# PSUM read-outs in streams of their own, and column tiles behind the scores, in a two-layer infini-attention kernel

## The chip, the cores and the metric

The kernel runs on one core of one Trainium2 chip. PSUM is the memory into which TensorE writes its products; it is divided into banks, and a bank is free for the next product when VectorE or ScalarE has read it out. The metric is device time in microseconds (us), the median over single executions. An execution counts as slow only where it is over 1.5% above the fastest of its kernel; the granted clock of TensorE is given with every execution. **Ratios** in this document are the mean time of one kernel's fast runs over the mean time of the fast runs of the kernel before in the same rounds on the same chip, with a 95% interval. They are therefore not quite the ratio of the medians quoted beside them. "Span" is the length of the one profiled execution, about 2 us shorter than its device time.

## The reference, cut to what matters

Two layers, each an attention with a compressive memory and a feed-forward part, over 2048 tokens of width 640; 32 heads of 20 columns, four segments of 512 tokens.

```python
for s in range(N):                                   # 4 segments
    logits = einsum('bhqd,bhkd->bhqk', qs, ks) * scale + mask
    p = softmax(logits)
    a_dot = einsum('bhqk,bhkd->bhqd', p, vs)          # scores, exponential, application
    pq = phi(qs)
    a_mem = einsum('bhld,bhde->bhle', pq, M) / (einsum('bhld,bhd->bhl', pq, z) + 1e-6)   # memory read
    outs.append(g * a_mem + (1 - g) * a_dot)
    M = M + einsum('bhld,bhle->bhde', phi(ks), vs)    # memory update
...
x = x + A(layernorm(x));  x = x + B(layernorm(x))     # B: relu(x @ w1) @ w2, width 1728
x = x + A(layernorm(x));  x = x + B(layernorm(x))
```

## The kernel before

The kernel's program is written as streams (Python generators): scores, exponentials, projections, feed-forward and so on. While the program is **built**, a small time model picks the next instruction of all streams, so the order on every engine is fixed before anything runs. TensorE has three tilings: "rows" for scores, "full" for a 128x128 product, and "cols" for the same product as four 128x32 column tiles. Which of the last two a product gets is decided here:

```python
def _mode(self, op):
    if op.cols is None:                  # scores: rows; application: cols; by token: full
        return op.mode
    return self.mode if self.mode != "rows" else "full"
...
if e == "pe":
    op.mode = self._mode(op)
    self.mode = op.mode
    if op.mode == "cols" and op.cols is not None:
        fns = op.cols                    # four matmuls instead of one
```

The model also charges a change of tiling (`SWITCH_NS = 96.0`) and, in full mode, ranks the application of the probabilities as if it came due 1.5 us after its inputs (`COLS_LAG`), so that it is put off. A product and its read-out from PSUM belong to one stream; the stream goes on when the read-out is recorded:

```python
def ffn(b, s):
    ...
    for dc in range(NFULL):
        bk, tk = yield from group(MISC, L, [(w1_r[:, k, ...], feat(xt, k)) for k in range(FC)], ...)
        th = yield evac(512, 1, ...relu on VectorE..., ...or on ScalarE..., [tk] + HT.tks)
        bk.release(th)
        hr.append(th)
```

Data that changes its layout goes over DMA: scores' operands (`pad<-scr`), and transposes such as `otk<-otu`, `phk<-phs`, `xnT<-xn_tok`, all issued from SyncE.

The softmax here doesn't subtract the row's maximum and nothing guards it: scores larger than these inputs give would overflow.

## Time and profile before

| | before |
|---|---|
| median, range | 557.86 us (557.83 to 558.56) |
| span of the profiled execution | 556.4 us |
| TensorE busy | 98%, 90% of the chain that ended last |
| matmuls, all instructions | 8,158, 18,717 |
| changes of tiling | 338 |

TensorE is busy in every slice, so what counts is the price of its stream and the holes in it. The prediction shows those lines. The page's DMA queues of the kernel before (packets, MB, share of the time of 16 DMA engines):

```profile
q1 hardware_dynamic: 129504, 59.62, 50.1%
...
q8 instruction: 64, 1.05, 0.8%
```

q8 fetches instructions: 64 packets of 16.4 KB. Their share, 0.8% of 16 x 556.4 us, is 71 us, so one packet holds one of the 16 DMA engines for about 1.1 us.

### The profile page before, as it was taken

The numbers are of one execution on the slowest core, as the hardware profiler recorded it, in microseconds if no ns is written. First come the engines' busy times: TensorE is split into PE (matmuls) and PEld (weight loads), VectorE is DVE, ScalarE is ACT, GpSimd is POOL, SyncE is SP. The second block draws the span as 40 slices with busy tenths as digits, with TensorE's granted clock in tenths as the row PEclk, the third lists the DMA queues.
The fourth block names the chain that finished last, engine by engine and source line by source line (L and its number), as shares of the span: only waits on it lengthen the run. The fifth ranks groups of instructions, "written<-read, shape, count | busy, mean of one in ns | idle before, by whom it ended". The sixth has DMA issues, their size and how long they took to land.

```text
span 556.4 us, 18717 instructions
## 1 busy us (share of the span) xinstructions
PE 546.7 (98%) x8158; PEld 307.7 (55%) x8158; DVE 414.3 (74%) x1063; ACT 405.9 (73%) x513; POOL 192.1 (35%) x302
## 2 busy tenths in 40 slices
PE   8998999999999999999999999999999999999998
PEld 7454554445554555645456554565465644657756
DVE  5967989979999988898577988779966588417102
ACT  5699888888777887787898887888774887541140
POOL 5345344433444434344334443244410433301000
PEclk9999999999999999999999999999999999999999
DMA  8596999845563427456187532771319311453101
GB/s 272 138 227 158 221 193 208 233 67 96 103 152 72 89 39 162 96 92 93 39 177 135 85 44 77 176 138 21 68 41 199 103 34 27 97 80 50 52 4 49
DMA packets 130003, 61.30 MB, mean 110 GB/s; under 512 B 108802, under 2 KB 119810, under 8 KB 129922
## 3 DMA queue, kind: packets, MB, share of 16 engines
q1 hardware_dynamic: 129504, 59.62, 50.1%
q8 instruction: 64, 1.05, 0.8%
q10 hardware_dynamic: 418, 0.49, 0.3%
q14 instruction: 17, 0.14, 0.1%
HBM read 20.57 MB, written 12.85 MB: 60 GB/s over the span
## 4 chain that ended last, share of the span: by engine, by line
PE 90%; DMA 4%; DVE 2%; ACT 1%; SPq 1%; issue 0%; POOL 0%; ACTq 0%; POOLq 0%
PE ps L645 45%; PE ps L648 24%; PE ps L1147 9%; PE ps L1241 6%; DMA otk<-otu 2%; PE ps L1280 1%; PE ps L1027 1%; DMA scr<-stg 1%; PE ps L1084 1%; PE ps L625 1%; ACT PT L1209 1%; PE ps L1421 1%; DMA pad<-scr 1%; DMA beta_bc<-in_A_beta_dram 1%; SPq L943 0%
## 5 line engine op out<-in xcount | busy, mean ns | idle before, releaser
L1209 ACT ACTIVATE PT<-ps 128x1024 bf16<-128x1024 f32 x320 | 309.3, 1027 | 66.2 <-PE ps L1147 62.9
L1221 POOL TENSOR_SCALAR_AFFINE_SELECT PT<-PT 128x512 bf16<-128x512 bf16 x256 | 166.7, 669 | 266.6 <-ACT PT L1209 266.5
L1363 DVE TENSOR_TENSOR x_sb<-x_sb,ps 128x320 bf16<-128x320 bf16 x128 | 60.8, 481 | 64.7 <-PE ps L648 47.1
L645 PE MATMUL ps<-w_r,hT 128*128 128x320 bf16 x511 | 82.2, 300 | 0.0
L645 PE MATMUL ps<-xnT,w_r 128*128 128x512 bf16 x262 | 65.7, 380 | 0.0
L1147 PE MATMUL ps<-pad 20*128 20x512 bf16 (+3 forms) x1024 | 63.4, 301 | 1.6 <-DMA pad<-scr 0.8
L648 PE MATMUL ps<-xnT,w_r 128*32 128x512 bf16 x1032 | 62.8, 379 | 0.8 <-issue 0.6
L645 PEld LDWEIGHTS ps<-w_r,hT 128*128 128x128 bf16 x511 | 47.6, 98 | 24.3 <-issue 6.8
L666 DVE BATCH_NORM_STATS2 stats<-x_sb 128x6 f32<-128x320 bf16 x124 | 55.4, 469 | 2.6 <-DMA x_sb<-in_A_x_dram 2.4
L648 PE MATMUL ps<-w_r,hT 128*32 128x320 bf16 x1284 | 49.2, 299 | 0.0
L1147 PEld LDWEIGHTS ps<-pad 20*128 20x128 bf16 x1024 | 17.9, 92 | 52.7 <-ACT PT L1209 26.9
L1450 ACT ACTIVATE hT<-ps 128x512 bf16<-128x512 f32 x50 | 30.0, 600 | 21.4 <-PE ps L648 20.4
L1448 DVE TENSOR_SCALAR hT<-ps 128x512 bf16<-128x512 f32 x54 | 37.0, 686 | 10.0 <-PE ps L645 6.6
L1241 PE MATMUL ps<-PT,v_aug 128*21 128x128 bf16 (+3 forms) x896 | 40.4, 301 | 0.0
L648 PEld LDWEIGHTS ps<-xnT,w_r 128*32 128x32 bf16 x1032 | 26.6, 97 | 22.8 <-issue 0.8
L648 PEld LDWEIGHTS ps<-w_r,hT 128*32 128x32 bf16 x1284 | 33.7, 97 | 9.7 <-DVE x_sb L1363 0.3
L1251 DVE CAST otu<-ps 128x512 bf16<-128x512 f32 x47 | 32.1, 684 | 8.5 <-PE ps L1241 8.1
L645 PEld LDWEIGHTS ps<-xnT,w_r 128*128 128x128 bf16 x262 | 23.4, 97 | 26.3 <-issue 3.5
L682 POOL TENSOR_TENSOR rstd<-lnU,mhalf 128x2 f32<-128x2 f32 (+2 forms) x26 | 20.4, 784 | 47.0 <-DVE lnU L678 37.5
L992 ACT ACTIVATE stg<-stg 128x512 bf16<-128x512 bf16 x50 | 31.6, 634 | 4.0 <-DVE rtmp L990 4.0
L645 PE MATMUL ps<-wo_r,oT 128*128 128x320 bf16 x202 | 32.3, 300 | 0.4 <-DVE x_sb L1363 0.4
L843 DVE CAST stg<-ps 128x512 bf16<-128x512 f32 x39 | 26.4, 683 | 7.8 <-PE ps L645 7.3
(108 smaller groups left out, 725.1 us busy)
## 6 DMA issues: line engine op xcount, KB each, us to landing
pad<-scr SPq DMA_DIRECT2D x124, 80.0 KB
scr<-stg SPq DMA_DIRECT2D x34, 256.0 KB, 2.7
out_dram<-x_sb SPq DMA_DIRECT2D x16, 160.0 KB, 2.0
w_r<-in_B_w_dram SPq DMA_DIRECT2D x10, 216.0 KB, 2.6
w_r<-in_B_w_dram SPq DMA_DIRECT2D x13, 160.0 KB, 2.8
x_sb<-in_A_x_dram SPq DMA_DIRECT2D x10, 160.0 KB, 3.4
scr<-w_r SPq DMA_DIRECT2D x5, 256.0 KB, 2.8
wv_r<-in_A_wv_dram SPq DMA_DIRECT2D x1, 800.0 KB, 8.8
```

The lines of the kernel that those rows point to most:

```text
L645: return e.matmul(view(dst.ap, b), a, b, start=(k == 0), stop=(k == last))
L648: return e.matmul(view(dst.ap[rows], b), part, b, start=(k == 0), stop=(k == last))
L666: tk = yield dve(320, 1, lambda e, c2=c2: e.bn_stats(stats6[:, t % 12, c2, :], x_sb[:, t, c2 * 320:(c2 + 1) * 320]), xt)
L992: te = yield act(512, lambda e, q=q: e.activation(q, q, ACT.Exp), [tr] + p, psum=False)
L1147: fns.append([(lambda e, z=z, j=j, hh=hh, N=N, o=o, sl=sl, q=hh % 2: e.matmul(slot.ap[:, q, o:o + N], sl.ap[32 * hh:32 * hh + DH, z, 0, 12 ...
L1209: tx = yield act(1024, lambda e, dst=dst, src=src: e.activation(dst, src, ACT.Exp, scale=SCALE), sc + pw)
L1221: tm = yield pool(600.0, lambda e, reg=reg: e.affine_select(out=reg, in_=reg, pattern=[[0, 4], [1, 128]], compare_op=ALU.is_ge, fill=0.0, ...
L1241: fns.append((lambda e, OD, j=j, hh=hh: e.matmul(OD.ap[32 * hh:32 * hh + DH + 1, 128 * j:L], VAUG[vx(a, s)][:, j, 4 * g + hh, :], pt.ap[:, ...
L1251: te = yield evac(L, 1, lambda e: e.tensor_copy(dst, OD.ap), lambda e: e.activation(dst, OD.ap, ACT.Copy), [tk] + OTU[0].tks)
L1363: ta = yield dve(320, 1, lambda e: e.tensor_tensor(x_sb[:, t, 320 * hf:320 * hf + 320], x_sb[:, t, 320 * hf:320 * hf + 320], bk.ap[:, 0:32 ...
L1448: th = yield evac(512, 1, lambda e, dc=dc, bk=bk: e.tensor_scalar(hT[:, dc, :], bk.ap[:, :], 0.0, None, ALU.max), lambda e, dc=dc, bk=bk: ...
L1450: lambda e, dc=dc, bk=bk: e.activation(hT[:, dc, :], bk.ap[:, :], ACT.Relu), [tk] + HT.tks)
```

## The change

The intent: with read-outs in streams of their own, a second product group can go into another bank while the first is being read out; and with cols behind scores, TensorE no longer turns from full to cols within one stretch between two score blocks. The core of the diff:

```diff
@@ _mode
-        return self.mode if self.mode != "rows" else "full"
+        return self.mode if self.mode != "rows" else "cols"
@@ _settle
+            if isinstance(y, Spawn):
+                self.add(y.prio, y.gen)
+                self.rank[id(y.gen)] = self.rank[id(st[1])]
+                st[2], st[3] = None, (None,)
@@ ffn
+            def square(dc, bk, tk):
+                th = yield evac(512, 1, ...)
+                bk.release(th)
+                S.set("hr", b, s, dc, tks=[th])
             for dc in range(NFULL):
+                if dc >= 2:
+                    yield Need(*hr[dc - 2])
                 bk, tk = yield from group(MISC, L, ...)
-                th = yield evac(512, 1, ...)
-                bk.release(th)
-                hr.append(th)
+                yield Spawn(6, square(dc, bk, tk))
```

Left out: the same for the query and key projections (`proj_part`), the values (`proj_v`) and the residual add behind the second feed-forward product. Projections and values may be two groups ahead only from the fourth segment on.

More of the change, by code (lines that the diff above doesn't have):

```diff
@@ L156, in __init__ @@
         self.key = key
+class Spawn:
+    def __init__(self, prio, gen):
+        self.prio = prio
+        self.gen = gen
 LONE_NS = 300.0
@@ L214, in _settle @@
                 return True
-            if isinstance(y, Need):
+            if isinstance(y, Spawn):
+                self.add(y.prio, y.gen)
+                self.rank[id(y.gen)] = self.rank[id(st[1])]
+                st[2], st[3] = None, (None,)
+            elif isinstance(y, Need):
                 if y.key not in self.events:
@@ L281, in run @@
                 moved = False
-                for st in self.streams:
+                for st in list(self.streams):
                     had, ended = st[2], st[4]
@@ L641, in group @@
             for k, (a, b, *w) in enumerate(mms):
-                w = list(w[0]) if w else []
+                if w and isinstance(w[0], Need):
+                    w = yield w[0]
+                else:
+                    w = list(w[0]) if w else []
                 def mm(e, dst, k=k, a=a, b=b):
@@ L842, in proj_part, with settle @@
                 (w_r[:, k, c * 128:(c + 1) * 128], feat(xt, k)[:, i0:i1]) for k in range(FC)], w)
-            te = yield evac(N, 1, lambda e, sg=sg, bk=bk: e.tensor_copy(sg.ap[:, t0:t0 + N], bk.ap[:, 0:N]),
-                            lambda e, sg=sg, bk=bk: e.activation(sg.ap[:, t0:t0 + N], bk.ap[:, 0:N], ACT.Copy),
-                            [tk] + sg.tks)
-            bk.release(te)
-            ev.append(te)
-            if len(ev) == (1 if h is None else 2):
-                S.set("stg", a, s, c, n, tks=ev)
+            def settle():
+                te = yield evac(N, 1, lambda e: e.tensor_copy(sg.ap[:, t0:t0 + N], bk.ap[:, 0:N]),
+                                lambda e: e.activation(sg.ap[:, t0:t0 + N], bk.ap[:, 0:N], ACT.Copy), [tk] + sg.tks)
+                bk.release(te)
+                ev.append(te)
+                S.set("qkpart", a, s, c, n, h)
+                if len(ev) == (1 if h is None else 2):
+                    S.set("stg", a, s, c, n, tks=ev)
+            yield Spawn(5, settle())
             return tk
@@ L854, in proj_first @@
             order += [(c, n, None) for c in range(2, FC) for n in range(2)]
-            for c, n, h in order:
+            for z, (c, n, h) in enumerate(order):
+                if z >= 1:
+                    c0, n0, h0 = order[z - 1]
+                    yield Need("qkpart", 0, 0, c0, n0, h0)
                 tk = yield from proj_part(0, 0, c, n, h)
@@ L865, in f @@
                 for c in range(FC):
+                    back = 2 if (a, s) >= (0,3) else 1
+                    if c >= back:
+                        yield Need("qkpart", a, s, c - back, n, None)
                     tk = yield from proj_part(a, s, c, n, None)
@@ L885, in proj_v, with settle @@
             done = []
+            def settle(i, hf, bk, tk):
+                dst = va.ap[:, i, 16 * hf:16 * hf + 16, 0:DH]
+                src = bk.ap[:, 0:320].rearrange("p (h e) -> p h e", e=DH)
+                te = yield evac(320, 1, lambda e: e.tensor_copy(dst, src), lambda e: e.activation(dst, src, ACT.Copy),
+                                [tk] + va.tks)
+                bk.release(te)
+                done.append(te)
+                S.set("vpart", a, s, 2 * i + hf)
+                if len(done) == 8:
+                    S.set("v", a, s, tks=done)
             for i in range(4):
@@ L888, in proj_v @@
                 for hf in range(2):
+                    back = 2 if (a, s) >= (0,3) else 1
+                    if 2 * i + hf >= back:
+                        yield Need("vpart", a, s, 2 * i + hf - back)
                     bk, tk = yield from group(MISC, 320, [
@@ L891, in proj_v @@
                         for k in range(FC)], [xtk[i % 2]] + wt)
-                    dst = va.ap[:, i, 16 * hf:16 * hf + 16, 0:DH]
-                    src = bk.ap[:, 0:320].rearrange("p (h e) -> p h e", e=DH)
-                    te = yield evac(320, 1, lambda e, dst=dst, src=src: e.tensor_copy(dst, src),
-                                    lambda e, dst=dst, src=src: e.activation(dst, src, ACT.Copy),
-                                    [tk] + va.tks)
-                    bk.release(te)
-                    done.append(te)
+                    yield Spawn(4, settle(i, hf, bk, tk))
             done_with(a, s, xt, tk)
-            S.set("v", a, s, tks=done)
         def spill(a, s):
@@ L1440, in ffn @@
             w1t = yield Need("w10")
-            hr = []
+            hr = [("hr", b, s, dc) for dc in range(NFULL)]
             tk = None
+            def square(dc, bk, tk):
+                th = yield evac(512, 1, lambda e: e.tensor_scalar(hT[:, dc, :], bk.ap[:, :], 0.0, None, ALU.max),
+                                lambda e: e.activation(hT[:, dc, :], bk.ap[:, :], ACT.Relu), [tk] + HT.tks)
+                bk.release(th)
+                S.set("hr", b, s, dc, tks=[th])
             for dc in range(NFULL):
+                if dc >= 2:
+                    yield Need(*hr[dc - 2])
                 if 128 * (dc + 1) > DFF // 2 >= 128 * dc:
@@ L1447, in ffn @@
                     (w1_r[:, k, dc * 128:(dc + 1) * 128], feat(xt, k)) for k in range(FC)], xtk + w1t)
-                th = yield evac(512, 1, lambda e, dc=dc, bk=bk: e.tensor_scalar(
-                    hT[:, dc, :], bk.ap[:, :], 0.0, None, ALU.max),
-                    lambda e, dc=dc, bk=bk: e.activation(hT[:, dc, :], bk.ap[:, :], ACT.Relu), [tk] + HT.tks)
-                bk.release(th)
-                hr.append(th)
+                yield Spawn(6, square(dc, bk, tk))
             HALF[b, s, 0] = tk
@@ L1457, in ffn, with residual @@
             hrest = yield Need("hR", b, s)
+            sums = [[] for _ in range(NJ)]
+            def residual(i, hf, bk, tk):
+                ta = yield from add_half(4 * s + i, hf, bk, tk)
+                S.set("sum", b, s, 2 * i + hf)
+                sums[i].append(ta)
+                if len(sums[i]) == 2:
+                    S.set("xB", b, s, i, tks=sums[i])
             for i in range(NJ):
-                t = 4 * s + i
-                tks = []
                 for hf in range(2):
                     cs = slice(hf * 320, (hf + 1) * 320)
+                    if 2 * i + hf >= 2:
+                        yield Need("sum", b, s, 2 * i + hf - 2)
                     bk, tk = yield from group(MISC, 320, [
-                        (hT[:, dc, i * 128:(i + 1) * 128], w2_r[:, dc, cs], [hr[dc]]) for dc in range(NFULL)] + [
+                        (hT[:, dc, i * 128:(i + 1) * 128], w2_r[:, dc, cs], Need(*hr[dc])) for dc in range(NFULL)] + [
                         (hR[:, (i % 2) * 128:(i % 2) * 128 + 128], w2_r[:, NFULL + i // 2, cs], hrest)], w2t)
-                    ta = yield from add_half(t, hf, bk, tk)
-                    tks.append(ta)
-                S.set("xB", b, s, i, tks=tks)
+                    yield Spawn(6, residual(i, hf, bk, tk))
             HT.release(tk)
```

## The prediction

> **What bounds the kernel now.** I read the page first (busy shares, slices, the chain that ended last), then the waits, then the timeline, and last every start-to-start distance between consecutive matmuls over the whole span.
>
> ```profile
> span 556.4 us, 18717 instructions
> ...
> PE 546.7 (98%) x8158; PEld 307.7 (55%) x8158; DVE 414.3 (74%) x1063; ACT 405.9 (73%) x513; POOL 192.1 (35%) x302
> ...
> PE   8998999999999999999999999999999999999998
> ...
> PE 90%; DMA 4%; DVE 2%; ACT 1%; SPq 1%; issue 0%; POOL 0%; ACTq 0%; POOLq 0%
> PE ps L645 45%; PE ps L648 24%; PE ps L1147 9%; PE ps L1241 6%; DMA otk<-otu 2%; PE ps L1280 1%; PE ps L1027 1%; DMA scr<-stg 1%; PE ps L1084 1%; PE ps L625 1%; ACT PT L1209 1%; PE ps L1421 1%; DMA pad<-scr 1%; DMA beta_bc<-in_A_beta_dram 1%; SPq L943 0%
> ```
>
> TensorE is the bound, in every slice and on 90% of the chain. VectorE and ScalarE have a quarter of the span spare. L645 is a product of a projection or of the feed-forward part as one 128x128 tile ("full"), L648 the same product as four 128x32 column tiles ("cols"); L1147 are the scores in row tiles ("rows"). So the question is not whether read-outs get faster but whether TensorE's stream gets shorter or loses holes. How few holes it has, the waits show (columns: who waited for whom, us in all, times, longest):
>
> ```profile
> ACT PT L1209 <- PE ps L1147: 62.9, 102, 3.6
> ...
> PE ps L625 <- POOL mhalf L575: 1.6, 1, 1.6
> ...
> PE ps L645 <- DVE w_r L843: 0.9, 1, 0.9
> ...
> PE ps L1147 <- DMA pad<-scr: 0.8, 1, 0.8
> ```
>
> ScalarE waits for scores 62.9 us, TensorE for anybody not even 2 us at one place. But ends of matmuls are modelled and overlap, so holes hide in "busy". I therefore sorted all start-to-start distances by the two forms they join and took the lower quartile of each kind as its price. The prices sum to 536.1 us, the actual distances to 551.7: **15.6 us of holes**, of which 2.2 lie in the first 40 us, 4.9 between 40 and 120, 1.3 between 240 and 280, 1.8 between 400 and 440, 1.7 after 480, and about 0.5 in each other 40 us. The stretch outside the matmuls (1.6 us before the first start, some 3 at the end for the last residual add and store) stays.
>
> **The prices**, in one stretch of the timeline (start, us from start to last end, what):
>
> ```profile
> 201.15 0.39 PE L648 MATMUL ps<-xnT,wk_r 128*32 128x512 bf16 x4
> 201.46 0.40 PE L1147 MATMUL ps<-pad 20*128 20x512 bf16 x4
> 201.79 0.39 PE L645 MATMUL ps<-xnT,wk_r 128*128 128x512 bf16 x1
> 202.02 0.84 PE L645 MATMUL ps<-wo_r,oT 128*128 128x320 bf16 x5
> 202.70 0.81 PE L645 MATMUL ps<-xnT,wk_r 128*128 128x512 bf16 x3
> 203.34 0.84 PE L645 MATMUL ps<-wo_r,oT 128*128 128x320 bf16 x5
> ...
> 205.17 0.85 PE L648 MATMUL ps<-wo_r,oT 128*32 128x320 bf16 x20
> 205.85 0.39 PE L648 MATMUL ps<-xnT,wk_r 128*32 128x512 bf16 x4
> ```
>
> Five full products of 320 columns take 202.70 - 202.02 = 0.68 us, 136 ns each; twenty quarter matmuls, which are the same five products, take 205.85 - 205.17 = 0.68 us too. With 512 columns: full 216 ns (median of 418), a set of four quarters 216 ns (median of 299). So four column tiles cost **nothing and save nothing** on a product. A change of tiling does cost: the four quarters at 201.15 are followed by rows after 0.31 us (median 312 ns) where another product would follow after 216: **+96 ns**. Over the whole trace full to rows is the same 312, and full (320) to cols is 229 instead of 136, **+93 ns**. Leaving rows costs 147 ns to full and 144 to cols after a 128-column score. I count 338 changes: 160 into rows, 160 out of them, and 18 from full to cols.
>
> **What the Trainium skill says.** "TensorE: Matmul & The Clock Gate", Back-to-back issue gap, gives N/2.4 + 2.5 ns for a warm stream; that is 136 and 216 ns, and the trace agrees in both tilings. "TensorEngine Tiling (Array Packing)", Key Properties, says that changing the tiling mode drains TensorE; the trace agrees, with the 93 to 96 ns above. The same page, Restrictions, says that column tiling excludes Fast Weight Load, which would be the danger of the change; the trace shows no price for it, as the quarter sets keep 136 and 216 ns (their weight loads hide behind the streams). "Runtime: NRT & Kernel Launch", Instruction fetch mechanics, says that instructions are streamed in blocks of 16 KiB; the page's 64 packets with 1.05 MB of instructions fit that, and matter below.
>
> **The change, part by part.**
> 1. *Cols behind the scores.* Before, a product after scores goes to full, and the tiling turns to cols when the application of the probabilities (L1241) or L1421 comes; now it goes to cols at once. That removes the 18 changes from full to cols: 18 x 93 ns = 1.7 us. It adds some: in the first segment the probabilities are applied by token (L1280) in full mode only. Of those nine blocks five follow scores directly, and four follow other products, which will now be cols: 4 x 94 ns = 0.4 us. Net **-1.3 us**. The 320 changes around 160 score blocks stay; that is where nearly all of the drain (30 us) is, and the change doesn't touch it. Leaving rows for cols instead of full saves 3 ns, about 120 times: **-0.4 us**.
> 2. *The memory update L1084.* In cols each quarter multiplies only its own heads (42 or 63 columns) except in the first token block. In the trace twelve full ones take 128.87 - 128.05 = 0.82 us, 66 to 68 ns each, and 24 quarters, six products, take 0.16 us, 27 ns each:
>
> ```profile
> 79.53 0.33 PE L1084 MATMUL ps<-w_r,phk 128*32 128x42 bf16 x24
> 79.69 1.03 PE L648 MATMUL ps<-hT,wk_r 128*32 128x512 bf16 x16
> ```
> ```profile
> 128.05 0.98 PE L1084 MATMUL ps<-v_aug,phk 128*128 128x147 bf16 x12
> 128.87 0.30 PE L645 MATMUL ps<-wv_r,xnT 128*128 128x320 bf16 x1
> ```
>
>    74 of the 120 products run full now; I leave a dozen in full (after by-token blocks) and count three quarters of the rest as cheaper: some 48 x 39 ns = **-1.9 us**. The memory read L1027 has no such gain (147 columns: 64 to 69 ns either way).
> 3. *Products themselves.* Without the outliers the full ones average 136.1 and 216.2 ns, the sets 135.8 and 215.7: about 900 x 0.3 + 540 x 0.5 ns = **-0.5 us**.
> 4. *Read-outs in their own streams.* Nothing is removed; VectorE and ScalarE do the same work, in another recorded order. A stream may put a second product group behind a first that is not yet read out (feed-forward always; projections and values only from the fourth segment on). That can only fill holes of TensorE. In the early part, where most of the 15.6 us lie, projections and values still wait for the group before, as now. Of the later 8 or so I give it 1 or 2: **-1.3 us** as a guess inside known limits.
>
> Sum: -1.3 - 0.4 - 1.9 - 0.5 - 1.3 = -5.4 us, 557.86 to **552.5 us**, about 1% less.
>
> **Rivals.**
> - *The order gets worse.* All PSUM is in use: four single banks serve all products and read-outs. If two groups per stream hold banks, the application of the probabilities finds none, the exponentials stall, and scores come late. For it: feed-forward work that is always ready is taken earlier, and filler could be missing at the transition around 420 us. Against it: TensorE never waits long for a bank today, and 72 us of pure feed-forward work remain after the last scores (481.4 us), so filler is plentiful. It would cost 3 to 8 us: 556 to 561, no gain left.
> - *The instruction stream becomes the bound.* Some 1,600 full products become four matmuls and four weight loads each, about 9,600 more instructions, half as many again, while the DMA engines are 76 to 80% busy in the first 120 us. For it: the only idle time before quarter sets without a named cause is 0.6 us. Against it: after 481 us the kernel runs 1,580 quarter matmuls in 64 us at undisturbed prices. If it bit in the early part: +2 to +6 us.
> - *The holes close much more.* If the new order removes half of them, the time is 546 to 549. Against it: the early ones are waits for data that still comes at its own time.
>
> **Range and chances.** Parts 1 to 3 are sure to about 1 us; the order of work is what spreads, by some 4 us either way, a bit more upward because of the first two rivals. Predicted 552.5, range 547.5 to 558.0. Faster by 2% means under 546.7: it needs two thirds of the reachable holes gone, 6%. Slower by 2% means over 569, for which no mechanism is in sight: 2%. Within 2%: 92%.
>
> **What would show it.** Right: no or hardly any change from full to cols left (rows to cols about 150 times, cols to full a handful), some 12,900 matmuls, prices of 136 and 216 ns unchanged, L1084 with 27 ns per product, holes of 12 to 16 us. Wrong: prices of quarter sets that rise in the early part (instruction stream, weight load); more score blocks or many by-token changes; holes that grow around 40 to 120 or 420 us, with TensorE waiting for read-outs (banks); or holes under 9 us, which would make read-out order the larger effect.

## The result, and the profile after

| | before | after |
|---|---|---|
| median of the same rounds | 558.02 us (557.83 to 558.56, 4 runs) | 563.95 us (562.65 to 565.04, 4 runs) |
| ratio | | 1.0104 (1.0079 to 1.0128), all at clock 1.0 |
| span | 556.4 us | 562.7 us |
| matmuls, all instructions | 8,158, 18,717 | 13,060, 28,522 |
| changes of tiling | 338 | 322 |

The change made the kernel about 1% **slower**: inside the 2% called "same", but outside the predicted range and with the other sign.

The page of the kernel after (span; busy time with instruction counts; TensorE's busy tenths; DMA queues; the chain that ended last by engine and by line; L661 is the quarter product, L658 the full one, L1177 the scores):

```profile
span 562.7 us, 28522 instructions
...
PE 544.8 (97%) x13060; PEld 318.7 (57%) x13060; DVE 411.0 (73%) x1053; ACT 412.7 (73%) x523; POOL 192.4 (34%) x302
...
PE   8989899999999999999999999999999899999998
...
q1 hardware_dynamic: 129504, 59.62, 52.4%
q8 instruction: 102, 1.67, 1.3%
...
PE 81%; DMA 8%; DVE 6%; ACT 2%; SPq 1%; issue 1%; POOL 0%; ACTq 0%; DVEq 0%
PE ps L661 63%; PE ps L1177 8%; PE ps L1271 5%; DMA phk<-phs 2%; DMA pad<-scr 2%; PE ps L1057 2%; ACT PT L1239 1%; DMA scr<-stg 1%; PE ps L658 1%; DMA otk<-otu 1%; PE ps L1114 1%; DVE stats L679 1%; DVE x_sb L1393 1%; DMA scr<-w_r 1%; PE ps L1451 1%; DVE phs L1023 1%
```

TensorE is busy for less time than before, in a longer span. On the chain TensorE falls from 90% to 81%, DMA rises from 4% to 8% and VectorE from 2% to 6%. The same 129,504 data packets take 52.4% of the DMA engines where they took 50.1% (4,720 us against 4,460 us), and 38 more instruction packets run beside them.

The waits after (who waited for whom, us in all, times, longest):

```profile
ACT PT L1239 <- PE ps L1177: 64.5, 100, 5.0
...
DVE rden L1357 <- DMA otk<-otu: 16.1, 11, 4.6
...
PE ps L1177 <- DMA pad<-scr: 2.9, 3, 1.9
...
PE ps L1177 <- ACT PT L1239: 1.8, 3, 1.0
```

and the one row of the kernel before's waits that the prediction doesn't show:

```profile
DVE rden L1327 <- DMA otk<-otu: 6.8, 8, 2.8
```

VectorE's wait for the transposed attention output rose from 6.8 to 16.1 us, and TensorE's wait for score operands from 0.8 to 2.9 us. A hole, in the timeline of TensorE after (start, us from start to last end, what, idle time before it):

```profile
434.35 0.44 PE L661 MATMUL ps<-w_r,hT 128*32 128x320 bf16 x8
434.62 0.44 PE L661 MATMUL ps<-wo_r,oT 128*32 128x320 bf16 x8
437.00 0.39 PE L1177 MATMUL ps<-pad 20*128 20x512 bf16 x4 [1.94 <-DMA pad<-scr]
```

And the prices, in another stretch of the same timeline:

```profile
299.60 0.65 PE L1114 MATMUL ps<-v_aug,phk 128*32 128x147 bf16 x48
300.06 1.69 PE L661 MATMUL ps<-w_r,hT 128*32 128x320 bf16 x44
...
302.14 0.86 PE L661 MATMUL ps<-w_r,hT 128*32 128x320 bf16 x20
302.83 0.71 PE L1271 MATMUL ps<-PT,v_aug 128*21 128x512 bf16 x16
```

Forty-eight quarters of the memory update, twelve products, take 0.46 us, where the kernel before took 0.82 us for twelve full ones. Five products of 320 columns in quarters still take 0.69 us. So the price of the work was as predicted; the holes were not.

**How holes are counted from here on.** The prediction took them matmul by matmul (15.6 us). To compare kernels with different tilings I now take a whole product, a whole score block or a whole application as one unit, pool the start-to-start distances of each kind over all runs (the two failed filler runs left out), call the lower quartile of a kind its price, and the excess over it a hole. The warm-up matmuls are left out. That gives, from the one profiled execution of each kernel:

```
                                         price    holes    fetches (q8)
before                                   535.2     11.1        64
after                                    532.9     20.5       102
after - before                            -2.3     +9.4
```

About 0.7 us of the +9.4 is an artefact of the start (in the kernel after the warm-up matmuls ran faster, so the same wait for the first transposed input shows as a hole). The rest, +6.4 us, is the longer span (+6.3). By stretches of 80 us the holes went 5.1, 2.5, 0.4, 1.1, 0.7, 1.3, 0.0 before and 9.0, 5.0, 0.8, 1.3, 1.3, 3.2, 0.0 after: they grow where the DMA engines are busiest and at the passage around 420 us, and not at all in the tail after 480 us.

Two more things lie in these holes. First, an execution can run a stretch in which TensorE is granted half of its clock, and what it loses there counts as a hole. The profiles of the kernel before, the kernel after, e2 to e7, e12 to e14 and e18 have no such stretch before their last matmul; those of e1, e8, e11, e15, e16 and e17 have nine, of 3.4 or 6.8 us, which hold 1.6, 3.0, 1.5, 6.5, 3.9 and 3.0 us of their holes. Second, the texts of what was expected still count as the prediction did, matmul by matmul; where they speak of prices of 526 us and holes of 27 or 28 us in the kernel after, they mean the 532.9 and 20.5 us of this table.

### The profile page after: what moved, and what is told of

Read it like the earlier page. It is cut to its first block, busy times and chain, and to the rows that moved or that the text cites. A ratio compares the mean times of both kernels' runs of the same rounds, so it can differ in the third digit from the quotient of the medians.

```text
span 562.7 us, 28522 instructions
## 1 busy us (share of the span) xinstructions
PE 544.8 (97%) x13060; PEld 318.7 (57%) x13060; DVE 411.0 (73%) x1053; ACT 412.7 (73%) x523; POOL 192.4 (34%) x302
## 3 DMA queue, kind: packets, MB, share of 16 engines
q1 hardware_dynamic: 129504, 59.62, 52.4%
## 4 chain that ended last, share of the span: by engine, by line
PE 81%; DMA 8%; DVE 6%; ACT 2%; SPq 1%; issue 1%; POOL 0%; ACTq 0%; DVEq 0%
PE ps L661 63%; PE ps L1177 8%; PE ps L1271 5%; DMA phk<-phs 2%; DMA pad<-scr 2%; PE ps L1057 2%; ACT PT L1239 1%; DMA scr<-stg 1%; PE ps L658 1%; DMA otk<-otu 1%; PE ps L1114 1%; DVE stats L679 1%; DVE x_sb L1393 1%; DMA scr<-w_r 1%; PE ps L1451 1%; DVE phs L1023 1%
## 5 line engine op out<-in xcount | busy, mean ns | idle before, releaser
L1239 ACT ACTIVATE PT<-ps 128x1024 bf16<-128x1024 f32 x320 | 309.0, 1024 | 67.1 <-PE ps L1177 64.5
L661 PE MATMUL ps<-w_r,hT 128*32 128x320 bf16 x3328 | 135.4, 299 | 0.1
L661 PE MATMUL ps<-xnT,w_r 128*32 128x512 bf16 x2080 | 127.2, 380 | 0.1
L661 PEld LDWEIGHTS ps<-w_r,hT 128*32 128x32 bf16 x3328 | 85.6, 97 | 29.3 <-issue 7.9
L661 PEld LDWEIGHTS ps<-xnT,w_r 128*32 128x32 bf16 x2080 | 51.3, 96 | 48.3 <-issue 6.5
L1177 PE MATMUL ps<-pad 20*128 20x512 bf16 (+3 forms) x1024 | 63.4, 301 | 6.0 <-DMA pad<-scr 2.9
L661 PE MATMUL ps<-wo_r,oT 128*32 128x320 bf16 x1280 | 52.6, 300 | 0.7 <-DVE x_sb L1393 0.7
L1177 PEld LDWEIGHTS ps<-pad 20*128 20x128 bf16 x1024 | 17.9, 92 | 58.3 <-ACT PT L1239 27.8
L695 POOL TENSOR_TENSOR rstd<-lnU,mhalf 128x2 f32<-128x2 f32 (+2 forms) x26 | 20.3, 780 | 69.6 <-DVE lnU L691 60.4
L661 PEld LDWEIGHTS ps<-wo_r,oT 128*32 128x32 bf16 x1280 | 32.2, 97 | 14.8 <-issue 3.2
L857 DVE CAST stg<-ps 128x512 bf16<-128x512 f32 x43 | 29.3, 684 | 14.8 <-PE ps L661 14.5
L661 PE MATMUL ps<-wv_r,xnT 128*32 128x320 bf16 x880 | 36.8, 300 | 0.0
L661 PE MATMUL ps<-xnT,wk_r 128*32 128x512 bf16 x540 | 34.8, 380 | 0.0
L661 PE MATMUL ps<-xnT,wq_r 128*32 128x512 bf16 x548 | 34.2, 380 | 0.0
L1271 PEld LDWEIGHTS ps<-PT,v_aug 128*21 128x21 bf16 x896 | 22.8, 93 | 17.7 <-POOL PT L1251 1.1
```

Source lines behind the costliest of these rows:

```text
L661: return e.matmul(view(dst.ap[rows], b), part, b, start=(k == 0), stop=(k == last))
L695: tk = yield pool(740, lambda e: e.tensor_tensor(rstd[:, sl], lnU[:, sl], mhalf[:, 0:n], ALU.pow), [tk] + h)
L857: te = yield evac(N, 1, lambda e: e.tensor_copy(sg.ap[:, t0:t0 + N], bk.ap[:, 0:N]), lambda e: e.activation(sg.ap[:, t0:t0 + N], bk.ap[:, ...
L1177: fns.append([(lambda e, z=z, j=j, hh=hh, N=N, o=o, sl=sl, q=hh % 2: e.matmul(slot.ap[:, q, o:o + N], sl.ap[32 * hh:32 * hh + DH, z, 0, 12 ...
L1239: tx = yield act(1024, lambda e, dst=dst, src=src: e.activation(dst, src, ACT.Exp, scale=SCALE), sc + pw)
L1271: fns.append((lambda e, OD, j=j, hh=hh: e.matmul(OD.ap[32 * hh:32 * hh + DH + 1, 128 * j:L], VAUG[vx(a, s)][:, j, 4 * g + hh, :], pt.ap[:, ...
```

## The experiments

Eighteen kernels ran, all with correct results. Theory **F** (fetches): more instructions mean more fetches of instructions, each of which holds one DMA engine for about a microsecond; transfers that need that engine land later, and since the order is fixed, TensorE waits. Theory **O** (order): the rule and the streams change the built order for the worse. Theory **L** (lag): the application is no longer put off by its 1.5 us in the model, because that slack is tied to full mode. (The first batch was planned before theory F; its texts call the streams S and the lag C.)

### Batch 1: the two parts alone, the tiling at an unchanged order, and a placebo

**e1_cols_alone**: the new rule in the kernel before, read-outs as before.
```diff
-        return self.mode if self.mode != "rows" else "full"
+        return self.mode if self.mode != "rows" else "cols"
```

> Kernel before with one word changed: after scores the products go to column tiles instead of the full tile; read-outs stay in their product's stream. Theory S (the read-out streams made the holes): prices fall by some 5 us, holes stay near 15 us, about 553 us. Theory C (column tiling made them, because the 1.5 us of slack that the application of the probabilities gets in full mode no longer applies): about 563 us, holes 25 us or more. Theory O (any other recorded order loses against this tuned one): 556 to 563 us, with holes scattered over other places than before.

Measured: 569.47 us (566.77 to 570.78) against 558.85, ratio 1.0182 (1.0149 to 1.0216). Price 536.0, holes 23.4. It is slower than each of the three theories of the text allows. TensorE waited 6.1 us for the exponential and 4.1 us for the residual add, against 0.8 and 0.4 us in the kernel before, so most of this loss is not one of transfers. The rule alone did more harm than the whole change; batch 4 shows how much of such a difference an order by itself can make.

**e2_streams_alone**: the kernel after with the old rule.
```diff
-        return self.mode if self.mode != "rows" else "cols"
+        return self.mode if self.mode != "rows" else "full"
```

> The changed kernel with the tiling rule of before: read-outs in streams of their own, products after scores in the full tile. Theory S: some 568 us, as the gain of the tiling (about 5 us of prices) is gone and the holes (about 27 us) stay. Theory C: 558 us or less, holes 15 us. Theory O: slower than before too, 560 to 568 us, holes 20 to 28 us, at other places than in the changed kernel.

Measured: 558.64 us (557.01 to 559.33), ratio 1.0000 (0.9978 to 1.0023). Price 535.3, holes 11.6. The streams alone neither gain nor lose.

**e3_old_order_in_cols**: the kernel before in exactly its own order on every engine, but all products behind the first scores are emitted in quarters.
```diff
+                self.scored = self.scored or op.mode == "rows"
-                if op.mode == "cols" and op.cols is not None:
+                if op.cols is not None and (op.mode == "cols" or self.scored):
                     fns = op.cols
```

> Kernel before, every engine's instructions in exactly the order of before, but all products behind the first scores emitted as four column tiles. It takes the price of the tiling by itself. All theories that blame the order: prices 526 us as in the changed kernel, holes 15 to 16 us as before, about 553 us (-1%). If quarter matmuls themselves bring holes (instruction stream, weight loads): 558 us or more, holes that grow in the first 120 us.

Measured: 561.76 us (560.45 to 565.37), ratio 1.0071 (1.0032 to 1.0109). Price 533.7, holes 17.6. The order being the same, theory O can't explain this: quarters by themselves save 1.5 us of price and open 6.5 us of holes. (1.2 us of the 6.5 are the artefact of the start: the last warm-up matmul began at 5.7 us here and at 6.9 us in the kernel before. The longer span, +3.8 us, agrees with 5.3 us of holes.) The page of this run:

```profile
span 560.2 us, 28863 instructions
...
PE 545.5 (97%) x13231; PEld 320.3 (57%) x13231; DVE 415.7 (74%) x1063; ACT 405.8 (72%) x513; POOL 191.7 (34%) x302
...
q8 instruction: 104, 1.70, 1.3%
...
PE 78%; DMA 11%; DVE 5%; ACT 3%; SPq 1%; issue 1%; POOL 0%; ACTq 0%; DVEq 0%
```

The fetches rose from 64 to 104, and DMA's share of the chain from 4% to 11%. Since instructions of both kernels can be paired one to one, one transfer can be followed. In the kernel before (view of the tile `otk`, 126 to 134 us; ns minimum/median/maximum, then first and last start in us):

```profile
L688 SPq DMA_TRANSPOSE otk<-otu x1: 1233/1233/1233, 127.1 to 127.1; - x1
L1327 DVE RECIPROCAL rden<-otk x1: 344/344/344, 131.3 to 131.3; 128x32 f32<-128x32 bf16 x1
```

and in e3:

```profile
L690 SPq DMA_TRANSPOSE otk<-otu x1: 1232/1232/1232, 128.1 to 128.1; - x1
L1329 DVE RECIPROCAL rden<-otk x1: 355/355/355, 133.2 to 133.2; 128x32 f32<-128x32 bf16 x1
...
  DVE rden L1329: 1.1, 1
```

From issue to use it was 4.2 us before, with no wait of VectorE, and 5.1 us in e3, where VectorE waited 1.1 us for it. In e3 a fetch ran from 130.8 to 132.2 us, within that time; in the kernel before the transfer had landed (130.3 us) when the next fetch began (131.1 us). All 145 transfers of SyncE whose landing both traces record, sorted by whether a 16.4 KB packet ran on some DMA engine during the transfer (from 0.9 us after its issue on):

```
met a fetch (before -> e3)   transfers   landing later, median   mean
no  -> no                        37             -2 ns             -8
no  -> yes                       55           +540 ns           +643
yes -> no                        14           -656 ns           -862
yes -> yes                       39           +237 ns           +441
all: met one 53 -> 94                         +104 ns           +277
```

A longer transfer is more likely to meet a fetch, so the second and third rows overstate the effect somewhat; the first row does not. Walking back e3's chain and comparing each start with its twin, the chain ends 3.8 us late: transfers with their issue on SyncE contribute +6.3 (`pad<-scr` 2.1, `otk<-otu` 1.7, the load of x 1.0, `phk<-phs` 0.9), TensorE itself -0.9, the other engines the rest.

**e4_placebo**: one assumed cost of the kernel before's time model moved by 3 ns.
```diff
-SWITCH_NS = 96.0
+SWITCH_NS = 93.0
```

> Kernel before with one constant of the recorder changed that should mean nothing: the assumed cost of a tiling change 93 instead of 96 ns. The recorded order differs from about the 166th row of TensorE on. Theories S and C: no reason for a difference, 557 to 559 us. Theory O: slower by 1 to 6 us, with new holes.

Measured: 559.08 us (558.73 to 559.44), ratio 1.0013 (0.9996 to 1.0029). Price 535.3, holes 12.7; transfers landed slightly earlier in the mean, by less than 0.1 us. Under the old rule another order costs about nothing, and about 1.5 us of holes is what mere chance does.

### Batch 2: the new order in the old tiling, spare traffic, and quarters only where they pay

**e5_new_order_in_full**: the kernel after's order, emitted by the old tiling rule.
```diff
+                if op.cols is None:
+                    self.told = op.mode
+                elif self.told == "rows":
+                    self.told = "full"
-                if op.mode == "cols" and op.cols is not None:
+                if self.told == "cols" and op.cols is not None:
```

> The changed kernel with every engine in exactly its order, but the products emitted under the old tiling rule (full after scores, cols only behind something that needs cols): 7,714 matmuls in place of 13,060, about 41 tiling changes more than before (some +4 us of prices). Theory F (the instruction fetches, 16 KiB packets of about 1 us that grew from 64 to 102, hold up other transfers on the DMA engines, and TensorE, whose order is fixed, waits for what they delay): holes fall from 28 to under 20 us, 557 to 561 us. Theory O (the recorded order is the bad thing): holes stay near 27 us, 566 to 569 us.

Measured: 567.35 us (567.19 to 568.55), ratio 1.0169 (1.0151 to 1.0188); 60 fetches, 379 changes of tiling, price 540.1, holes 14.8. The time is in the range that the text gives to theory O. But 4.9 us of it are price: this order was built for cols and pays in changes when run full. Its holes, which lie between the two forecasts, complete a table of order by tiling:

```
holes, us                     old tiling      quarters      quarters cost
before's order                11.1            17.6 (e3)         +6.5
streams' order, old rule      11.6 (e2)       18.3 (e12)        +6.7
the new order                 14.8 (e5)       20.5 (after)      +5.7
```

In each pair the run in quarters also has the artefact of the start, of 1.2, 0.9 and 0.8 us (last warm-up matmul at 5.7, 6.1 and 6.2 us against 6.9, 7.0 and 7.0). Without it quarters cost 5.3, 5.8 and 4.9 us of holes, **some 5 to 6 us in each order**; the new order costs another 3 to 4. Comparing e5 with the kernel after, 55 transfers newly met a fetch (+495 ns, median), 25 no longer did (-927 ns); the mean of all rose by only 101 ns.

**e6_40_packets** and **e7_120_packets**: the kernel before with 40 or 120 spare transfers of 8,192 elements within DRAM, issued by ScalarE, evenly spread.
```diff
+        for z in reversed(range(40)):        # e7: 120
+            ...
+            P.ops["act"].insert(k + 1, ("op", lambda e, z=z, src=src: e.dma_start(spare[z:z + 1, :], src), dsp, 16))
```

> Kernel before, order and tiling untouched, plus 40 transfers of one 16 KiB piece from one place of the main memory to another, evenly spread over ScalarE's queue: as many as the changed kernel fetches more instructions. Theory F: 3 to 8 us slower, holes 19 to 23 us, and a median transpose transfer that takes 0.3 to 0.9 us longer. If the fetches are harmless: 558 to 559 us, as ScalarE only has 40 issues more.

> The same with 120 such transfers. Theory F: more than with 40, some 8 to 15 us slower than before. Otherwise within 2 us of before.

Measured: e6 559.00 us (558.51 to 559.94), ratio 1.0012 (0.9992 to 1.0032), holes 12.5; e7 560.37 us (559.60 to 560.66), ratio 1.0037 (1.0020 to 1.0055), holes 12.7. Both looked like a blow to theory F, until the trace showed that they were not the intended test: each spare transfer had been cut into 16 pieces of 1,024 bytes that took 46 ns each (median), so none held an engine for a microsecond. Batch 4 repeats it.

**e8_cols_where_needed**: the kernel before's order; a stretch between two score blocks is in quarters as a whole if it holds an operation that exists in cols only or a memory update, and full as a whole if not.
```diff
+def retile(P, log):
+    ...
+        cols = z > 0 and not any(x[0] == "full" for x in st) and (
+            z == len(stretches) - 1 or any(x[0] == "cols" or x[1] for x in st))
+    ...
         S.run()
+        retile(P, S.log)
```

> Kernel before in its order; between two score blocks all products are in cols only if something there needs cols or is a memory update, otherwise all are full. 320 tiling changes, no full to cols, memory updates in quarters, 9,214 matmuls, so only some 8 fetches more than before. Prices fall by 3 to 4 us; theory F: holes grow by at most 2 us, 555 to 557 us, faster than both kernels. Theory O agrees (same order), 554 to 555 us. If quarters as such cost something: 558 us or more.

Measured: 557.16 us, ratio 1.0005 (0.9971 to 1.0039); 9,214 matmuls, 320 changes, 72 fetches, price 531.9. Four of six executions took 556.68 to 557.29, one 559.84 and one, the profiled one, 563.14 with a mean clock of 0.994 and holes of 18.9. Windows of that profile (us, then busy time and count of PE, PEld, DVE, ACT and POOL, granted clock, DMA share, GB/s):

```profile
35.00:38.00 3.00, 1.95 (x78) 1.54 (x78) 1.11 (x4) 1.97 (x3) 1.74 (x3) 0.98 1.04 216
38.00:41.00 3.00, 3.00 (x43) 1.22 (x29) 1.77 (x3) 2.72 (x4) 1.25 (x3) 0.50 1.00 267
```

After a stretch in which TensorE was busy 1.95 of 3 us, it ran at half its clock for 3 us. Seven of the nine stretches at half clock in the profiles follow a distance of 1.1 to 2.2 us between two matmuls within some 4 us; but the hole of 1.9 us in the kernel after, shown above, was followed by none, so that holes cause them is not shown. They explain only a part of the spread between executions: 3.4 us at half clock lower the mean clock of an execution to 0.997 and, as an estimate from that length, lose at most 1.7 us.

### Batch 3: fillers, the lag, and the streams' order in quarters

**e9_sp_fillers** and **e10_pe_fillers**: to add fetches without touching the tiling, thousands of instructions that wait on semaphores that are already satisfied, in SyncE's idle time (9,844 more than before) or ahead of TensorE's full products (6,532 more).
```diff
+            if e == "pe" and op.cols is not None and op.mode == "full" and len(fns) == 1 and self.P.cnt["dve"]:
+                self.P.ops[e] += [("wait", self.P.clk["dve"], 1)] * 9
```

> Kernel before with some 9,840 waits that are already met, put into SyncE's stream where it idles for over 1.2 us, in number so that they fit there. TensorE's stream is untouched. It adds about as many instructions as the changed kernel has more, but another engine fetches them. Theory F (instruction fetches delay transfers, whoever fetches): transfers that meet a fetch land 0.3 to 1 us later, holes 18 to 24 us, 560 to 565 us. If only TensorE's own fetches or quarter matmuls matter: 558 to 559 us.

> Kernel before with some 6,530 waits that are already met in TensorE's own stream, ahead of the full products: no more matmuls, same order, some 25 more instruction fetches (65 to about 89; the old order in cols had 104). Theory F: prices unchanged (136 and 216 ns, if the waits are hidden behind the streams), holes up by about 5 us, 561 to 564 us. If it is the quarter matmuls and not the fetches: 558 to 559 us with holes of 15 to 17 us. If the waits are not hidden, prices rise and the run is no test.

Measured: 879.13 us (ratio 1.574) and 1003.37 us (ratio 1.797). Both failed as tests: such an instruction costs 61 ns on SyncE and 106 ns on TensorE from start to start (medians), although its record lasts 28 and 51 ns, so the fillers delayed their own engines. They say nothing on F.

**e11_lag_kept**: the kernel after, with the application's slack in the model in cols too.
```diff
-        if not op.lag or self.mode != "full":
+        if not op.lag or self.mode == "rows":
```

> The changed kernel with the 1.5 us of slack for the application of the probabilities kept in cols mode (it applies in every mode but rows). Theory L (the order got worse because this slack went with full mode): holes fall from 28 to about 24 us, 559 to 561 us. If the slack is not the cause: 562 to 566 us.

Measured: 565.86 us (563.99 to 567.48), ratio 1.0128 (1.0089 to 1.0166), holes 20.3, as in the kernel after. Keeping the slack gains nothing in this build. That speaks against theory L, but the edit makes another order too, and batch 4 shows how far orders under the new rule scatter.

**e12_streams_old_rule_in_cols**: the order of e2 exactly, in quarters, by the same edit as e3.
```diff
+                self.scored = self.scored or op.mode == "rows"
+                if op.cols is not None and (op.mode == "cols" or self.scored):
```

> The order of the run with read-out streams alone (558.6 us), emitted in cols behind the first scores: a third pair of one order in both tilings. From the other two pairs: holes up by 8 us (15 to 23), prices down by some 5 us (532 to 527), 560 to 563 us. If streams of their own make an order that bears cols better: 556 to 558 us.

Measured: 564.63 us (563.22 to 568.37), ratio 1.0129 (1.0085 to 1.0173); 104 fetches, price 533.9, holes 18.3 against 11.6 in e2. It repeats e3 in a second order: +257 ns in the mean over 189 transfers, 65 of which met a fetch in e2 and 115 in e12, and +908 ns for the 71 that newly met one. Its chain ends 4.4 us later than e2's, transfers contributing +5.8.

### Batch 4: spare transfers in one piece, and placebos under the new rule

**e13_40_whole_pieces** and **e14_120_whole_pieces**: e6 and e7 with one element less per transfer, which keeps it in one piece on one DMA engine.
```diff
-        spare = nc.dram_tensor("spare", [40, 8192], dt.bfloat16, kind="Internal").ap()
+        spare = nc.dram_tensor("spare", [40, 8191], dt.bfloat16, kind="Internal").ap()
```

> As the run with 40 spare transfers, but of 8,191 elements in place of 8,192: the length no longer divides, so each goes as one piece of 16,382 bytes on one DMA engine, as an instruction fetch does, and not as 32 pieces of 512 bytes. The places, the issues on ScalarE and the bytes are the same; TensorE's stream is that of before. Theory F: identical transfers that meet such a piece land 0.4 to 1 us later, holes grow by 3 to 7 us over before, 561 to 565 us. If a held DMA engine is not what matters: 559 us, as with the split transfers.

> The same with 120 whole pieces. Theory F: clearly more, 566 to 578 us. Otherwise 560 us, as with 120 split ones.

(Where the first text speaks of 32 pieces of 512 bytes, the trace of e6 has 16 of 1,024 bytes, each followed by a semaphore write.) Measured: e13 560.45 us (558.82 to 561.87), ratio 1.0025 (1.0006 to 1.0044), holes 13.2; e14 566.43 us (563.29 to 568.89), ratio 1.0132 (1.0099 to 1.0164), holes 18.0. The queue of the spare transfers on the page of e7 (the kernel before has 418 packets and 0.3% there):

```profile
q10 hardware_dynamic: 4258, 2.47, 1.9%
```

and on that of e14:

```profile
q10 hardware_dynamic: 658, 2.46, 1.5%
```

Both move the same bytes; e7's small pieces even take more of the DMA engines' time (1.9% against 1.5%). What differs is the length of a piece, 0.85 us (median) in e14, and slightly the issue on ScalarE, 546 against 496 ns each. Yet e7 costs about 2 us and e14 about 7. Tiling, order and prices of TensorE are those of the kernel before in both, so **long packets on single DMA engines alone open holes in TensorE**, of the size that quarters do:

```
                  mean later landing    transfers that met a long packet    holes, us
e6   40 split          +54 ns                  70 -> 71 of 189                12.5
e7  120 split          +67 ns                  70 -> 70 of 189                12.7
e13  40 whole         +137 ns                  62 -> 90 of 174                13.2
e14 120 whole         +227 ns                  62 -> 132 of 174               18.0
e3   40 fetches       +277 ns                  53 -> 94 of 145                17.6
```

What doesn't fit count for count is e13: 40 whole pieces cost 1.4 us of time and 2.1 us of holes, the 40 added fetches of e3 5.3 us of holes without the artefact of the start (0.4 us in e14). A spare piece holds its engine 0.85 us and a fetch 1.1 us, fetches come when TensorE runs through many quarters, not evenly, and a part of e3's holes is TensorE's own (see the rival that was dismissed); whether that covers the gap no run shows.

**e15_placebo_on_new** and **e16_second_placebo_on_new**: the kernel after with that assumed cost at 93 and 100 ns.
```diff
-SWITCH_NS = 96.0
+SWITCH_NS = 93.0        # e16: 100.0
```

> The changed kernel with the recorder's assumed cost of a tiling change 93 in place of 96 ns. If the 3 to 4 us of holes that the new order adds come from one decision of the new rule, it stays at 562 to 566 us. If they are the luck of one order among many, it may fall anywhere from 558 to 568 us.

> The same with 100 ns. Both readings as for the other; the spread of the three orders under the new rule is the answer.

Measured: e15 569.46 us (564.89 to 571.11), ratio 1.0176 (1.0142 to 1.0210), holes 26.0; e16 558.49 us (557.59 to 561.51), ratio 0.9992 (0.9975 to 1.0009), holes 16.5. Under the new rule the order is a lottery: 558.5, 564.0 and 569.5 us from 100, 96 and 93 ns of one assumed cost, where the old rule gave 558.0 to 559.1 in three orders (before, e2, e4). So theory O holds for the other 3 to 4 us; that they are the luck of this build is likely from three builds, not certain. Which decision of the new order costs them stays open. (Both profiles are of the slowest execution, with 6.5 and 3.9 us of their holes in stretches at half clock; outside them 19.5 and 12.6 us are left.) e16 also limits theory F: with 102 fetches and 13,054 matmuls it is as fast as the kernel before. What fetches cost depends on the order too, and the 5 to 6 us hold for the three orders that ran in both tilings.

### Batch 5: few quarters in the streams' order

**e17_streams_cols_where_needed**: e2's order with e8's rule. **e18_cols_where_needed_again**: e8 unchanged, once more on the same chip.
```diff
-        return self.mode if self.mode != "rows" else "cols"
+        return self.mode if self.mode != "rows" else "full"
...
         S.run()
+        retile(P, S.log)
```

> The order of the run with read-out streams alone (558.6 us), with cols only in those stretches between score blocks that hold something that needs cols or a memory update. 320 tiling changes, 9,277 matmuls, about 9 fetches more than before. Prices fall by some 3 us; if holes grow only as landings get later, by 1 to 2 us: 556 to 558 us. If any quarter set costs as much as in the full conversion: 560 us or more.

> The same kernel as the first run with cols where needed, to settle its unclear verdict (556.7 to 563.1 us there). If its two slow executions were rare: median 556 to 557.5 us, under before by 1 to 2 us. If not, 558 to 560 us.

Measured: e17 556.79 us (556.23 to 560.13), ratio 0.9972 (0.9943 to 1.0000), 320 changes; e18 558.25 us (555.48 to 564.53), ratio 1.0017 (0.9970 to 1.0063), with two executions of 562.12 and 564.53 at clock 0.997; the latter counts as slow and is left out of the ratio. Of e18's two readings, it is the second that came true. The page of e17:

```profile
span 558.4 us, 20949 instructions
...
q8 instruction: 73, 1.20, 0.9%
```

With 73 fetches the price falls by 3.2 us (535.2 to 532.0). The profile of e17 is of its slowest execution (560.13, clock 0.994, holes 16.4); that of e18's fastest (555.48, clock 1.0) has a price of 531.8 and holes of 11.5. So all of the gain in price can be had without most of the fetches, but it is half a per cent of the time at best, and the holes scatter. e17 has the lowest median of all, with an interval that touches 1; it is a gain of 0.3% on the border of the noise, not a version that clearly beats both.

## Why the prediction was wrong

**Part 1, changes of tiling: right, one term mis-sized.** No change from full to cols is left (18 were counted), cols to full happens twice, and 322 changes remain. Leaving rows costs 3 ns less, as predicted. But I gave quarters and full one price on the way into rows: my 312 ns for quarters ran from the start of the last quarter, while the first had started 9 ns earlier (321 ns in the same trace), and I compared it with the 216 ns from first to first. Over the runs a set of quarters takes 320 ns (512 columns) and 241 (320 columns) from its first start to the scores, a full product 311 and 231: 9 ns more. Quarters leave for rows 141 times instead of 41, which gives back 100 x 9 ns = 0.9 us.

**Part 2, memory update: right.** Its price fell from about 6.8 to 4.9 us, -1.9 as predicted.

**Part 3, products: a size that was not there.** The 0.5 us from averages without outliers does not appear: both tilings keep their price per product. With the 0.9 us above, the price of TensorE's stream fell by 2.3 us, where parts 1 to 3 add up to 4.1; the last 0.4 us of the difference are not assigned.

**Part 4, holes: this is the step that failed.** "That can only fill holes of TensorE ... I give it 1 or 2: -1.3 us." They grew by 9.4 (8.7 without the artefact of the start): some 5 us because products run as quarters, 3 to 4 us because of the new order. The sentence looked at the streams alone, and for them it was nearly right: e2 shows no change. It took for granted that a product in quarters, which costs TensorE the same, costs nothing else, and that a new order can only fill holes.

**The rival that was dismissed.** "The instruction stream becomes the bound ... If it bit in the early part: +2 to +6 us." The amount was right, the mechanism and the argument against it were not. I asked whether TensorE would starve for instructions and looked at the tail, where 1,576 quarters run undisturbed (from 489 us on, not from 481 as I wrote). They do in the kernel after as well: no holes after 480 us. But in the tail hardly any transfer is waited for. Where transfers are waited for, the fetch hurts **others**. The evidence: at three fixed orders quarters open 4.9 to 5.8 us of holes; transfers that meet no fetch in either of two kernels land at the same time (medians of -2, +12 and +17 ns in the three pairs); the chain's lateness in e3 and e12 is that of transfers; and e14 makes holes of the same size with long packets and no quarter added. What remains argued, not shown, is that fetches are the whole of those 5 to 6 us, because e13's 40 pieces did less than 40 fetches.

A smaller part is TensorE's own, which the argument against the rival had ruled out. In the kernel after, TensorE stops within a score block, behind the first of eight weight loads, with no wait on record (start, us, what, idle time before it):

```profile
442.54 0.09 PEld L1177 LDWEIGHTS ps<-pad 20*128 20x128 bf16 x1 [0.27 <-issue]
...
443.45 0.40 PE L1177 MATMUL ps<-pad 20*128 20x256 bf16 x8 [0.84 <-issue]
443.45 0.12 PEld L1177 LDWEIGHTS ps<-pad 20*128 20x128 bf16 x7 [0.82 <-issue]
```

Three such stops take 1.4 us of the holes in the kernel after, three 1.7 us in e12, two 0.6 us in e3; in the kernel before, e2 and e5 none takes more than 0.1 us (the 0.6 us without a named cause that the prediction mentions stands before a product that waits for a transfer). Each of the eight ended 1.3 to 1.7 us after a packet of q8 had ended. That they are waits for TensorE's own instructions is likely from that; no run was made to show it.

The Trainium skill, "DMA: Bandwidth & Descriptors", Queues, rings and completion order, says that each DMA engine takes turns between its queues at packet granularity, draining a whole packet before switching. The difference between e7 and e14 agrees with that: equal bytes, about 2 against 7 us. "Runtime: NRT & Kernel Launch", Instruction fetch mechanics, calls the cost of crossing a 16 KiB boundary "mostly hidden". For TensorE's own stream the trace agrees in the main (prices per product unchanged at 13,060 matmuls, stops of 1.4 us in all); for the transfers beside it, it doesn't.

**The first rival, a worse order,** came true in part: 3 to 4 us, within its "3 to 8". Its given mechanism, read-outs that hold the banks, has only a small part in the waits: TensorE's waits for the residual add, a read-out, rose from 0.4 to 1.7 us, those for the exponential from 0.8 to 1.8 us, those for transfers (`pad<-scr`, `phk<-phs`, `hT<-xn_tok`) from 0.8 to 5.0 us, and e2 has the streams without the loss. I had also called the order's spread "some 4 us either way"; under the new rule three builds span 11 us.

## What to carry to other kernels

Count what a change does to the number of instructions, and if DMA engines are busy and transfers are on or near the critical path, price the added fetches by what they delay and not only by whether the issuing engine starves. In a kernel whose order is fixed at build time, run the same edit at one fixed order in both forms, and a placebo of the order, before believing any difference of a per cent. Use column tiles only where they save a change of tiling or work, not everywhere because a product costs the same.

## What the Trainium skill lacked or had wrong

- "Runtime: NRT & Kernel Launch", Instruction fetch mechanics: "mostly hidden" nearly holds for the engine that fetches, not for others. Fetches rose from 64 to 104 (about 1.1 us each on one DMA engine), transfers that newly met one landed 540 ns later (median of 55), and holes rose from 11.1 to 17.6 us at an unchanged order, 1.2 us of it an artefact of the start.
- "DMA: Bandwidth & Descriptors": it gives the rule of turns, not its price for a latency-bound kernel. 120 transfers of 16 KB in one piece cost about 7 us, the same bytes in pieces of 1 KiB about 2 us.
- "TensorEngine Tiling (Array Packing)": that a change of tiling drains is there, but not that leaving column tiles for row tiles costs more than leaving a full tile: 241 and 320 ns against 231 and 311.
- None of the pages that I used: the price of an instruction that waits on a semaphore that is already satisfied, 61 ns on SyncE and 106 ns on TensorE from start to start, with a record of 28 and 51 ns.
